# Turned attention rows on VectorE, zeroing from ScalarE's queue, and a plain last write, in a fused attention and mixture-of-experts kernel

## The chip, the cores and the metric

One core of one Trainium2 chip runs the whole program. The metric is the device time of one execution in microseconds (us); the time before is the median of three executions, 692.43 us (691.93 to 693.0).

## What is computed

Decayed linear attention (4 batches, 8 heads, 768 positions, head size 64) gives 3072 tokens of 512 features; each token is then sent to its two best of eight experts, and the two results are added with weights.

```python
for b in range(nb):                       # blocks of 64 positions, per batch and head
    intra = (einsum('bhic,bhjc->bhij', qb, kb) * Dmask) @ vb
    inter = (qb * lam_pow) @ kv_state
    out[b] = intra + inter
    kv_state = lam_block * kv_state + (kb * rev_pow).T @ vb
x = out as [3072, 512]
noisy = x @ w_gate + log1p(exp(x @ w_noise)) * noise
top2, w = two largest of noisy, softmax over the two
for e in range(8):
    out[mask_e] += w_e * (relu(x[mask_e] @ w1[e]) @ w2[e])
```

All arrays are float32. The kernel keeps that precision in the experts by splitting each operand into a high and a low part and adding three products (high·high, high·low, low·high).

## The kernel before, in words

**Attention.** Twelve steps (`for t in range(NST)`), each for two chunks of 128 tokens (tile `a` 0 and 1). A step on TensorE (PE) is, in this order: `products(t-1)` (the gate's logits, L425), `turn_x(t-1)` (L437), `trans_k(t+1)` (L321), `trans_q(t+1)` (L334), `kv(t+1)` (state update, L409), `intra(t)` and `inter(t, 0)` (L377), `scores(t+1)` (L364). PSUM has four rotating buffers called `pS` for transposes, states and scores. ScalarE (ACT) copies the turned keys and queries out (L323, L337), scales the keys (`kdecay`, L349) and copies the outputs out (`evac_o`, L397, into `XO`, features on partitions). VectorE (DVE) multiplies the scores with the decay mask (L367) and the queries with theirs (L341), adds the states (L417), and from step 4 on runs the routing (`routing`), a list of small instructions dealt out by `advance`.

`turn_x(u)` turns the outputs `XO[u]`, which have features on the partitions, into rows of tokens `XC[u]`: eight 128x128 transposes on PE (L437) and two copies by ACT (L438). `store_x(u)` writes these rows to `x_tok` in DRAM, by one DMA of 512 KB on GpSimd's queue for u below 8 and on SyncE's (SP) queue after that (L443). The inputs come by SP's queue: six loads of 256 KB a step (`load`, L160), for keys (`kt`, two buffers), queries (`qt`, two) and values (`vt`, three). A load of step t+3 stands in the program behind the use that frees its buffer in step t. Between them stand the first expert's weights (`load_w`, L770; `LOADS`), which here are in one or two DMAs each of 512 KB. SP's, ACT's and GpSimd's queues are served by the same 16 DMA engines.

**Zeros.** The experts after the first add into `out`, and tokens are written in scattered rows, so `out` is zeroed first by two DMAs on SP's queue (`zero_out`, L1152): 2 MB at step 11 and 4 MB after the first part of expert 0.

**Experts.** Expert 0 runs in three parts of tiles (`PARTS0`); each part is eight first-layer groups (L1037, evacuated by ACT L1043 and DVE L1047) and then the second layer tile by tile (`gemm2`, L1078). Meanwhile GpSimd (POOL) scatters the lists of tokens (`scatter_list`, L634); then SP reads the lists of the next expert back (`load_rec`, L880) and POOL gathers its rows of `x_tok` (`gather_rows`, L889), which PE turns (`trans_rows`, L898). Experts 2 to 7 gather rows, turn them 32x32 on DVE (`turn_rows`, L915) and pass them through DRAM; they form the first layer from seven products of half blocks. Every tile's rows leave through `scatter_out` (L1135): an indirect DMA on POOL's queue, which writes for expert 0 and adds in DRAM for the others. `gemm2` scales the rows on DVE right ahead of it (L1094). After the last tile a loop over overflow tiles follows, which has no turns here.

The order of all engines is the order of the code (`manual_schedule`); waits follow from the data.

## Time and profile before

| what | value |
|---|---|
| median of three executions | 692.43 us |
| the profiled execution: its time, its span | 693.23 us, 691.4 us |
| PE busy, of the span | 671.6 us, 97% |
| DVE, ACT, POOL busy | 482.4, 309.5, 370.0 us |
| DMA | 115.06 MB, mean 166 GB/s |
| granted TensorE clock, mean | 0.994 of full |

Three stretches are to be told apart: the attention (0 to about 140 us), the experts (140 to 683.5 us) and the end (683.5 to 691.4 us, in which PE has nothing left). A busy PE is the bound only where nothing else is busy all the time as well; for the attention the DMA row of the profile has to be read beside it. The profiled execution took 0.80 us more than the median.

### The profile page before, as it was taken

How to read it: one execution, taken by the hardware profiler on the slowest of the kernel's cores; microseconds unless marked ns; L12 is line 12 of the kernel's file. 1: busy time of each engine (PE TensorE's matmuls, PEld its weight loads, DVE VectorE, ACT ScalarE, POOL GpSimd, SP SyncE). 2: the span in 40 equal slices, each digit the busy share in tenths (PEclk: the TensorE clock that was granted, in tenths of full speed). 3: DMA queues.
4: the chain of work that ended last, by engine and by line, in shares of the span. 5: the costliest groups of instructions: out<-in, count | busy, mean ns of one | idle time of the engine just before them, and what ended most of it. 6: DMA issues, size and time to landing. Idle time of an engine off the chain costs nothing.

```text
span 691.4 us, 13961 instructions
## 1 busy us (share of the span) xinstructions
PE 671.6 (97%) x4861; PEld 598.1 (87%) x4861; DVE 482.4 (70%) x1060; ACT 309.5 (45%) x634; POOL 370.0 (54%) x474
## 2 busy tenths in 40 slices
PE   7899999899999999999999999999999999999995
PEld 4788888698898898899989998998898899889984
DVE  6335888878436566789867886889596979588610
ACT  2667786441133332365437434653363356327400
POOL 7111355678854555776358536753773667264332
PEclk9999999999999999999999999999999999999998
DMA  9999999576517437766477547854875576464033
GB/s 205 214 233 262 229 252 250 163 245 163 113 32 221 136 119 171 175 177 191 149 183 188 189 149 178 221 175 142 166 235 158 126 195 189 122 135 116 1 46 40
DMA packets 151901, 115.06 MB, mean 166 GB/s; under 512 B 88063, under 2 KB 123007, under 8 KB 151828
## 3 DMA queue, kind: packets, MB, share of 16 engines
q1 hardware_dynamic: 137636, 84.04, 44.8%
q0 software_dynamic: 13776, 29.57, 20.5%
q8 instruction: 39, 0.64, 0.4%
q10 hardware_dynamic: 416, 0.53, 0.3%
q14 instruction: 34, 0.28, 0.1%
HBM read 77.58 MB, written 37.32 MB: 166 GB/s over the span
## 4 chain that ended last, share of the span: by engine, by line
PE 68%; DVE 12%; issue 8%; POOL 4%; DMA 3%; SPq 2%; ACT 1%; POOLq 1%; DVEq 0%
PE pS L993 15%; PE pKV L1078 13%; PE pO L1078 10%; PE pS L1037 7%; PE pS L1110 5%; PE pS L364 3%; PE pKV L377 2%; POOL lst L634 2%; PE pO L377 2%; SPq L160 2%; PE pR L993 1%; POOL out_dram L1135 1%; DMA xr<-x_tok,rec 1%; DVE ht L1004 1%; PE pS L437 1%
## 5 line engine op out<-in xcount | busy, mean ns | idle before, releaser
L993 PE MATMUL pS<-xa,w 128*128 128x400 f32 (+1 forms) x624 | 158.0, 343 | 0.3 <-ACT gt L1012 0.2
L818 POOL TENSOR_TENSOR wst<-wst 128x256 f32<-128x256 f32 x96 | 96.4, 1016 | 84.1 <-DVE w L810 81.7
L993 PEld LDWEIGHTS pS<-xa,w 128*128 128x128 f32 x624 | 113.2, 188 | 4.6 <-DVE w L810 2.0
L1135 POOL DMA_INDIRECT out_dram<-ot,rec x40 | 73.6, 1839 | 75.5 <-DVE ot L1094 56.2
L1078 PE MATMUL pKV<-w2h,ht 128*128 128x512 f32 x336 | 109.0, 394 | 0.0
L1078 PE MATMUL pO<-w2h,ht 128*128 128x512 f32 x336 | 108.4, 392 | 0.0
L993 PE MATMUL pS<-xb,w 128*128 128x400 f32 (+1 forms) x240 | 81.6, 340 | 0.0
L1078 PEld LDWEIGHTS pKV<-w2h,ht 128*128 128x128 f32 x336 | 63.2, 188 | 14.3 <-DVE gt L1094 0.6
L1078 PEld LDWEIGHTS pO<-w2h,ht 128*128 128x128 f32 x336 | 63.1, 188 | 13.5
L1037 PE MATMUL pS<-xa,w 128*128 128x256 f32 (+2 forms) x440 | 73.5, 316 | 0.8 <-DVE xa L901 0.4
L1037 PEld LDWEIGHTS pS<-xa,w 128*128 128x128 f32 x440 | 65.3, 189 | 4.9 <-DVE xa L901 0.6
L1078 PE MATMUL pKV<-w2l,ht 128*128 128x512 f32 x168 | 65.8, 391 | 0.0
L1078 PE MATMUL pO<-w2l,ht 128*128 128x512 f32 x168 | 65.7, 391 | 0.0
L961 ACT ACTIVATE xa<-wst 128x512 fp32r<-128x512 f32 (+1 forms) x48 | 25.1, 568 | 79.5 <-DVE wst L970 72.3
L810 DVE TENSOR_TENSOR w<-wst,w 128x512 fp32r<-128x512 f32 (+2 forms) x72 | 59.6, 844 | 0.1
L889 POOL DMA_INDIRECT xr<-x_tok,rec x42 | 46.2, 1101 | 19.2 <-issue 6.5
L634 POOL DMA_INDIRECT lst<-recs,dest x48 | 49.7, 1035 | 10.8 <-issue 8.5
L1012 ACT ACTIVATE ot<-pS 128x400 f32<-128x400 f32 (+1 forms) x60 | 29.7, 495 | 48.8 <-PE pS L993 44.6
L808 ACT ACTIVATE w<-wst 128x512 fp32r<-128x512 f32 (+2 forms) x72 | 48.1, 692 | 5.3 <-POOL wst L818 5.2
L1004 DVE SCALAR_TENSOR_TENSOR ht<-ot,ht 128x400 fp32r<-128x400 f32 (+1 forms) x60 | 45.4, 756 | 1.5 <-ACT ht L1001 0.8
L993 PEld LDWEIGHTS pS<-xb,w 128*128 128x128 f32 x240 | 45.0, 188 | 0.6 <-DVE xb L962 0.3
L1043 ACT ACTIVATE ht<-pS 128x256 fp32r<-128x256 f32 (+2 forms) x40 | 17.9, 448 | 59.5 <-PE pS L1037 58.2
(287 smaller groups left out, 1367.0 us busy)
## 6 DMA issues: line engine op xcount, KB each, us to landing
wst<-in_moe_w_dram SPq DMA_DIRECT2D x36, 512.0 KB, 5.4
wst<-in_moe_w_dram SPq DMA_DIRECT2D x32, 256.0 KB, 3.3
kt<-in_k_dram SPq DMA_DIRECT2D x24, 256.0 KB, 5.6
qt<-in_q_dram SPq DMA_DIRECT2D x24, 256.0 KB, 6.7
vt<-in_v_dram SPq DMA_DIRECT2D x24, 256.0 KB, 5.3
wst<-in_moe_w_dram SPq DMA_DIRECT2D x48, 128.0 KB, 3.4
wst<-turned SPq DMA_DIRECT2D x96, 64.0 KB, 2.0
turned<-w1b SPq DMA_DIRECT2D x20, 256.0 KB, 2.8
```

The source lines that it names most:

```text
L634: st = nc.gpsimd.indirect_dma_start(out=lst, out_offset=bass.IndirectOffsetOnAxis(ap=r["dest"][:, i, c:c + 1], axis=0), in_=r["rec"][:, c, ...
L808: nc.scalar.activation(hi[:, ks], src, AF.Copy)
L810: nc.vector.tensor_tensor(lo[:, ks], src, hi[:, ks].bitcast(FT), op=SUB)
L818: g.tensor_tensor(o, x, y, op=op)
L889: nc.gpsimd.indirect_dma_start(out=xrow(e, t)[:size(e, t)], out_offset=None, in_=x_tok[:rows, :], in_offset=bass.IndirectOffsetOnAxis(ap=a ...
L993: nc.tensor.matmul(p, WO[f % 2][:, a, kw, d, :], xo(x, kx, kx + 1)[:, 0, d, :w], start=first and i == 0, stop=i == 5, skip_group_check=True)
L1004: return lambda: nc.vector.scalar_tensor_tensor(hv(e, 1, i, k), src, 0.0, hv(e, 0, i, k).bitcast(FT), op0=OP.max, op1=SUB)
L1012: nc.scalar.activation(banks[m], U, AF.Copy)
L1037: nc.tensor.matmul(p, W1[a][d][:, fs], xt(b, cs)[:, d], start=(d == 0 and i == 0), stop=(d == DB - 1 and i == 2))
L1078: nc.tensor.matmul(p, h, W2[b][f // 2][:, f % 2, :], start=(i == 0), stop=(i == len(TERMS) - 1))
L1110: nc.tensor.matmul(p, W2[b][f // 2][:, f % 2, d * 128:(d + 1) * 128], h, start=(i == 0), stop=(i == len(TERMS) - 1))
L1135: st = nc.gpsimd.indirect_dma_start(out=out, out_offset=bass.IndirectOffsetOnAxis(ap=REC[e, t][:, 0:1], axis=0), in_=o, in_offset=None, bo ...
```

## The change

Five things are changed together.

1. For the first four steps (`BLOCKS = 4`) `turn_x` turns 32x32 blocks on DVE instead of 128x128 on PE. A row of `XC` then lies on 32 partitions at a time with features in the order (32-block, head pair, feature), and `store_x` writes it by four DMAs of 32 partitions with pieces of 512 bytes instead of one DMA with rows of 2 KB. The later steps still use PE, and ACT's copy writes the same new order.
2. `x_tok` so has its features in another order. The first expert's weights are loaded to match: `load_w` takes four DMAs of 32 rows each where it took one or two. `turn_rows` reads its input without a reordering.
3. `out` is zeroed by twelve DMAs of 512 KB on ACT's queue, one behind each first-layer evacuation of expert 0's second part (eight) and the first four of its third part, in place of the two on SP's queue.
4. Ahead of expert 7's second layer POOL gathers the rows of `out` that its last tile will add to, into the tile `zero`.
5. The last tile is scaled and added to these rows on DVE (one SCALAR_TENSOR_TENSOR for one TENSOR_SCALAR) and is then written by an indirect DMA that doesn't add.

```diff
--- before.py
+++ after.py
@@ -67,8 +67,8 @@
 LOADS = {2: [(1, 0)], 3: [(1, 1)], 4: [(1, 2)], 5: [(1, 3)], 9: [(2, 0), (2, 1)], 10: [(2, 2)], 11: [(2, 3)]}
 HIGH = {4: [(1, 0)], 5: [(1, 1)], 6: [(1, 2)], 7: [(1, 3)], 10: [(2, 0), (2, 1)]}
 LOW = {5: [(1, 0)], 6: [(1, 1)], 7: [(1, 2)], 10: [(2, 0)]}
-ZEROS = {11: 8}
 LATE = (6, 7)
+BLOCKS = 4
 MID = 16
 X1 = ((), (), (), (), (0, 1), (2, 3, 4), (5, 6))
 WARM = (10, 1, 1)
@@ -430,18 +430,28 @@
 
     def turn_x(u):
 
-        XC[u] = aw.tile([128, 2, DB, C], FT, name="xc")
+        XC[u] = aw.tile([128, 2, DM], FT, name="xc")
         for a in range(2):
+            if u < BLOCKS:
+                nc.vector.transpose(XC[u][:, a].rearrange("p (i d c) -> p i d c", d=DB, c=32),
+                                    XO[u][:, a].rearrange("p d (i c) -> p i d c", c=32))
+                continue
             p = bank()
             for d in range(DB):
                 nc.tensor.transpose(p[:, d, :], XO[u][:, a, d, :], identf)
-            nc.scalar.activation(XC[u][:, a], p, AF.Copy)
+            nc.scalar.activation(XC[u][:, a].rearrange("p (i d c) -> p d i c", d=DB, c=32),
+                                 p.rearrange("p d (i c) -> p d i c", c=32), AF.Copy)
 
     def store_x(u):
 
         queue = nc.gpsimd if u < NST - 4 else nc.sync
+        if u < BLOCKS:
+            for i in range(4):
+                queue.dma_start(sub(x_tok, 2 * u * C * DM + i * 128, [[DM, 32], [32 * DM, 2 * DB], [1, 128]]),
+                                XC[u][i * 32:(i + 1) * 32].rearrange("p a (i x) -> p (a i) x", x=128))
+            return
         queue.dma_start(x_tok[2 * u * C:2 * (u + 1) * C, :].rearrange("(a p) m -> p a m", a=2),
-                          XC[u].rearrange("p a d i -> p a (d i)"))
+                        XC[u])
 
     def logits(u):
         nonlocal pl
@@ -764,10 +774,9 @@
     def load_w(which, e, j, queue=nc.sync):
         st = next(stage)
         if which == 1:
-            for s in range(2 if j % 2 else 1):
-                r = half(s) if j % 2 else slice(0, 128)
-                src = w1[EXP[e], j * 128 + (64 - r.start if j % 2 else 0):, :][:, :r.stop - r.start, :]
-                queue.dma_start(st[r, None, :], src.rearrange("e p f -> p e f"))
+            for d in range(DB):
+                at = d * 128 + (j ^ 2 * (d % 2)) * 32
+                queue.dma_start(st[d * 32:(d + 1) * 32, None, :], w1[EXP[e], at:at + 32, :].rearrange("e p f -> p e f"))
         else:
             src = w2[EXP[e], j * 256:(j + 1) * 256, :]
             queue.dma_start(st.rearrange("p (e a m) -> p e a m", e=1, a=2),
@@ -913,7 +922,7 @@
         else:
             tr = (zero, WX[0][:, :DM], WX[0][:, DM:])[next(place) % 3][:n, :]
         nc.vector.transpose(tr.rearrange("p (i d c) -> p i d c", d=DB, c=32),
-                            xrow(e, t)[:n, :].rearrange("p (d i c) -> p i d c", d=DB, c=32))
+                            xrow(e, t)[:n, :].rearrange("p (i d c) -> p i d c", d=DB, c=32))
         nc.sync.dma_start(turned[t % 3 if t < NT - 1 else 3][t // 3 % 2, :n, :], tr)
 
     def xturned(t):
@@ -1056,6 +1065,7 @@
 
     ahead = []
     OT = []
+    LAST = E - 1, tile_order(E - 1)[-1]
 
     def ring():
         OT.append(OT.pop(0))
@@ -1091,7 +1101,10 @@
             p = o
         if e in CROSS and n == TS:
             o, p = o.rearrange("p (b d c) -> p b d c", b=DB, c=32), p.rearrange("p (d b c) -> p b d c", b=DB, c=32)
-        nc.vector.tensor_scalar(o, p, w, None, op0=MULT)
+        if (e, t) == LAST:
+            nc.vector.scalar_tensor_tensor(o, p, w, zero, op0=MULT, op1=ADD)
+        else:
+            nc.vector.tensor_scalar(o, p, w, None, op0=MULT)
         if e:
             scatter_out(e, t, o if n < TS or e not in CROSS else o.rearrange("p b d c -> p (b d c)"))
 
@@ -1134,7 +1147,7 @@
         nc.gpsimd.memset(spacer, 0.0)
         st = nc.gpsimd.indirect_dma_start(
             out=out, out_offset=bass.IndirectOffsetOnAxis(ap=REC[e, t][:, 0:1], axis=0), in_=o, in_offset=None,
-            bounds_check=NTOK - 1, oob_is_err=False, **({"compute_op": ADD} if e else {}))
+            bounds_check=NTOK - 1, oob_is_err=False, **({"compute_op": ADD} if e and (e, t) != LAST else {}))
         if t == 0:
             out_st.clear()
         for s in out_st:
@@ -1149,8 +1162,8 @@
     def zero_out(n):
         i = list(itertools.islice(zeros, n))
         if i:
-            nc.sync.dma_start(out[i[0] * 128:(i[-1] + 1) * 128, :].rearrange("(a p) m -> p a m", p=128),
-                              zero[:, None, :].to_broadcast([128, len(i), DM]))
+            nc.scalar.dma_start(out[i[0] * 128:(i[-1] + 1) * 128, :].rearrange("(a p) m -> p a m", p=128),
+                                zero[:, None, :].to_broadcast([128, len(i), DM]))
 
     for t in range(NST):
         u = t + 1
@@ -1169,7 +1182,7 @@
             kv(u)
         if t:
             store_x(t - 1)
-            paced(1, XC[t - 1][:, 1, 0, :])
+            paced(1, XC[t - 1][:, 1, :])
         if t not in LATE:
             kdecay(t + 2)
         if u == NST:
@@ -1204,7 +1217,6 @@
         advance(FILLA.get(t, 18))
         for which, j in LOADS.get(t, []):
             load_w(which, 0, j)
-        zero_out(ZEROS.get(t, 0))
         if t == 2:
             turn_noise()
         if t == 4:
@@ -1256,6 +1268,8 @@
                     finish(2, False)
             if i or f >= 2:
                 paced(1 + (i == 2), ht(0, 0, f, columns(0, t0, n)).bitcast(FT))
+            if i:
+                zero_out(2)
             if i == 1 and f == 2:
                 load_rec(0, 1)
             if i == 2 and f == 2:
@@ -1270,7 +1284,6 @@
                 for j in X1[f - 4]:
                     trans_rows(j, size(1, j))
         if i == 0:
-            zero_out(NTOK // 128)
             advance(50)
         if i == 1:
             which_expert(1, nc.sync)
@@ -1472,6 +1485,10 @@
             step, todo = first_layer(e)
         if e == E - 1:
             nc.gpsimd.drain()
+            nc.gpsimd.indirect_dma_start(
+                out=zero, out_offset=None, in_=out,
+                in_offset=bass.IndirectOffsetOnAxis(ap=REC[LAST][:, 0:1], axis=0),
+                bounds_check=NTOK - 1, oob_is_err=False)
         if e == 1:
             WX.append(wp.tile([128, F], FT, name="w1b"))
             XB.append(hp.tile([128, 6 * 2 * HW], FR, name="xb"))
```

How this moves instructions, at the places that the prediction speaks of. On PE, at the start of an attention step (here the second; `identf` is the identity, `xo` the outputs, `kt` and `qt` keys and queries):

```order
 L377 MATMUL pO<-qTs,S_171 64x128
 L425 MATMUL pR<-xo,wgn 32x256 x4
-L437 MATMUL pS<-identf,xo 128x128 x8
 L321 MATMUL pS<-identf,kt 128x128 x8
 L334 MATMUL pS<-identf,qt 128x128 x8
```

The eight transposes of the outputs are gone, and those of the keys follow the gate's products directly. On DVE, at the same place:

```order
 L367 TENSOR_TENSOR at<-pS,Mk_130 128x512
 L367 TENSOR_TENSOR at<-pS,Mk_131 128x512
+L436 STREAM_TRANSPOSE xc<-xo 128x512 x2
 L341 TENSOR_TENSOR qTs<-pS,QS 128x4x128 x2
 L417 TENSOR_TENSOR S_174<-S_174,pS 128x256
```

Two transposes stand between the masks of the scores and the scaling of the next queries. On POOL, the stores of the first rows between the state updates (S):

```order
 L416 TENSOR_TENSOR S_172<-S_171,QS 128x256
 L416 TENSOR_TENSOR S_173<-S_172,QS 128x256
 L416 TENSOR_TENSOR S_174<-S_173,QS 128x256
-L443 DMA x_tok<-xc 128x2x512
+L450 DMA x_tok<-xc 32x8x128 x4
 L416 TENSOR_TENSOR S_171<-S_170,QS 128x256
```

Each store is four issues in the place of one. On POOL, ahead of expert 7's second layer, before:

```order
L818 TENSOR_TENSOR wst_161<-wst_161 128x2x128 x4
L818 TENSOR_TENSOR wst_162<-wst_162 128x2x128 x4
L846 TENSOR_TENSOR w2l_323<-wst_164,w2h_319 128x1024
L1134 MEMSET spacer 1x1
L1135 DMA out_dram<-ot_2377,rec_6565 3072x512
```

and in the changed kernel:

```order
L827 TENSOR_TENSOR wst_161<-wst_161 128x2x128 x4
L827 TENSOR_TENSOR wst_162<-wst_162 128x2x128 x4
L855 TENSOR_TENSOR w2l_323<-wst_164,w2h_319 128x1024
L1488 DMA zero<-out_dram,rec_6569 128x512
L1147 MEMSET spacer 1x1
L1148 DMA out_dram<-ot_2358,rec_6567 3072x512
```

The gather of the last tile's rows of `out` stands ahead of the expert's first write.

## Rows read from the trace of the kernel before

**Rows 1.** Busy us of each engine in stretches (start:end, length), instructions, PE clock, DMA share, GB/s.
```profile
30.00:40.00 10.00, 10.00 (x156) 8.76 (x155) 4.10 (x7) 7.27 (x20) 0.76 (x1) 1.00 1.08 237
120.00:130.00 10.00, 9.24 (x156) 7.85 (x156) 9.09 (x37) 5.71 (x10) 4.94 (x12) 1.00 0.39 123
130.00:140.00 10.00, 6.74 (x86) 5.28 (x82) 7.14 (x29) 4.03 (x8) 7.91 (x15) 1.00 0.74 241
140.00:150.00 10.00, 10.00 (x100) 9.91 (x101) 6.77 (x27) 5.46 (x12) 6.62 (x9) 1.00 0.66 161
190.00:200.00 10.00, 10.00 (x68) 9.83 (x66) 2.98 (x9) 1.85 (x5) 8.26 (x19) 1.00 0.33 59
```

**Rows 2.** Chain of work that ended last, 36 to 50 us (start, us, what).
```profile
37.80 0.57 PE pR L425 x8
38.37 1.02 PE pS L437 x8
```

**Rows 3.** By line: a DVE block transpose, ACT's and POOL's part in turned rows (ns).
```profile
L915 DVE STREAM_TRANSPOSE w1b<-xr 128x512 f32<-128x512 f32 x20 | 13.9, 696 | 0.0
...
L438 ACT ACTIVATE xc<-pS x24: 592/597/598, 29.6 to 142.5; 128x512 f32<-128x512 f32 x24
...
L443 POOL DMA_DIRECT2D x_tok<-xc x8: 733/742/794, 30.9 to 105.3; - x8
```

**Rows 4.** DMA, 20 to 110 us: queues (packets, MB, share), issues (KB, us to landing).
```profile
q1 hardware_dynamic: 58968, 16.91, 90.8%
q0 software_dynamic: 1307, 4.69, 15.9%
...
vt<-in_v_dram SPq DMA_DIRECT2D x19, 256.0 KB, 4.9
```

**Rows 5.** SP's queue: loads in order of issue (start, us), 59 to 64 and 92 us.
```profile
59.50 2.20 SPq L770 DMA_DIRECT2D wst<-in_moe_w_dram  x2
61.81 1.45 SPq L160 DMA_DIRECT2D kt<-in_k_dram  x2
63.36 4.11 SPq L160 DMA_DIRECT2D qt<-in_q_dram  x2
...
91.94 1.50 SPq L160 DMA_DIRECT2D vt<-in_v_dram  x1
```

**Rows 6.** Timeline, step 8: PE's first state product, and DVE's next masks.
```profile
101.78 0.34 PE L409 MATMUL pS<-vt,kd 128*64 128x64 f32 x4
...
106.95 2.48 DVE L367 TENSOR_TENSOR at<-pS,Mk 128x512 f32<-128x512 f32 x4 [0.56 <-PE pS L364]
```

**Rows 7.** The end: timeline from 682.5 us, and the last write's us to landing.
```profile
683.15 0.40 PE L1078 MATMUL pKV<-w2h,ht 128*128 128x512 f32 x1
683.58 0.75 DVE L1094 TENSOR_SCALAR ot<-pKV,rec 128x512 f32<-128x512 f32 x1 [4.74 <-PE pKV L1078]
684.61 1.56 POOL L1135 DMA_INDIRECT out_dram<-ot,rec  x1 [3.90 <-DVEq L1520]
...
out_dram<-ot,rec POOLq DMA_INDIRECT x1, 4.5
```

**Rows 8.** Indirect writes that don't add (xb), all landings on out, a DVE form.
```profile
L1135 POOL DMA_INDIRECT out_dram<-xb,recz x5: 985/998/1890, 230.9 to 241.8; - x5
...
DMA to landing us min/median/max: 2.7/5.1/7.6
...
out_dram<-xb,recz POOLq DMA_INDIRECT x5, 3.6
...
L1047 DVE SCALAR_TENSOR_TENSOR ht<-pS,ht 128x512 fp32r<-128x512 f32 x8 | 5.5, 692 | 9.7 <-ACT ht L1043 9.7
```

**Rows 9.** Gather at 207 us (chain), PE's wait for it, issues of zeros.
```profile
207.65 3.47 DMA xr<-x_tok,rec
...
PEld pS L898 <- DMA xr<-x_tok,rec: 0.3, 1, 0.3
...
L1152 SPq DMA_DIRECT2D out_dram<-zero x2: 520/698/877, 132.8 to 148.8; - x2
```

## The prediction

> **What bounds the kernel now.** I read first the table of busy time by stretches [rows 1], then the chain of waits through one attention step [rows 2], then the DMA queues and SP's issues [rows 4, 5], and last the end of the timeline [rows 7]. From 30 to 40 us PE is busy 10.00 of 10.00 us, at the full clock (1.00), while DVE has 4.10, ACT 7.27 and POOL 0.76; a reader would stop there and call the attention bound by PE. The DMA share in the same row is 1.08, though, and SP issues its loads one behind the other with next to nothing between (59.50 + 2.20 = 61.70, the next at 61.81; + 1.45 = 63.26, the next at 63.36) [rows 5]. So PE and the DMA engines are both full there: loads are not issued when a buffer comes free but when the queue takes them. From 120 to 140 us the row changes: PE has 9.24 and 6.74 of 10, DVE 9.09 and 7.14; routing on DVE paces the end of the attention. From 140 us PE is at 10.00 again. Then only the last 8 us are without PE: its last product starts at 683.15 and takes 0.40; DVE's scaling (0.75), POOL's part of the write (1.56) and its landing follow [rows 7], and the span ends at 691.4 us.
>
> **PE in four steps.** The eight transposes L437 are 1.02 us of the chain in a step [rows 2]. Four steps lose them: 4 x 1.02 = 4.1 us off PE. What comes in their place lies beside PE. DVE gets two block transposes of 0.696 us a step [rows 3], 1.4 us on an engine with 4.10 of 10 busy; they stand ahead of the next queries' scaling, which waits for PE's transposes anyway. ACT loses two copies of 0.597. POOL issues four DMAs where it issued one: 3 x 0.742 = 2.2 us more a step, on an engine with 0.76 busy [rows 1, 3]. What waits behind them on POOL is the next step's state update, several us away. If this cover were missing, the most it could cost is the 1.4 us of DVE a step.
>
> **The loads.** Steps that are shorter by 1.02 us want their inputs earlier, and the DMA engines have no time to give. The latest one I take is the second half of the values for step 8's product: issued at 91.94 [rows 5], landing 4.9 us later by the median of these loads [rows 4], so at 96.84; PE takes it at 101.78 [rows 6]. That is 4.94 us of margin, and PE will want it 4.1 us earlier, at 97.68. Alone, that still fits.
>
> But the change also gives the DMA engines more to do before that. The stores of rows now move 512-byte pieces instead of 2 KB ones. No row shows such pieces written, so I bound them. GpSimd's queue moved 4.69 MB in 15.9% of 16 engines over 90 us [rows 4], that is 90 x 0.159 = 14.3 us of all engines, or 1.60 us for a store of 0.524 MB. SP's queue with its 256-byte pieces took 0.908 x 90 = 81.7 us for 16.91 MB, or 2.53 us for 0.524 MB. A store of 512-byte pieces costs between the two, 0 to 0.93 us more. By a line through the time of a piece (256 bytes: 81.7 x 16 / 58968 = 22 ns; 2 KB: 14.3 x 16 us over 4.69 MB / 2048, 100 ns) a 512-byte piece takes 33 ns, 1024 of them on 16 engines 2.1 us: 0.5 us more, an estimate. Four stores give 2.1 us (bounds 0 and 3.7). The load then lands at 96.84 + 2.1 = 98.9 and PE, which wants it at 97.7, waits 1.3: of 4.1 us, **2.8 us** stay.
>
> The Trainium skill has a rule against this estimate ("DMA: Bandwidth & Descriptors", section Specifications): transfers in pieces of 512 bytes or more run at line rate, and only below that is there a read-modify-write. By it the four stores would cost nothing more and the full 4.1 us would stay. No run here shows such pieces yet.
>
> The split of the first expert's weights into four DMAs adds 10 issues on SP in these steps (6 before, 16 now). With bytes and row length unchanged I take them at nothing, because an issue there mostly waits for the queue; if each adds what a free issue costs (0.52 us, the least of the zeroing rows [rows 9]), it is 5.2 us, and the loads would take the whole gain. That is the other bound.
>
> The shift then has to pass the stretch where DVE paces. At 106.95 DVE still waits 0.56 us for PE's scores [rows 6], so it is not behind there, and all it does after that moves with PE. From 140 us on PE is full and carries the shift to the end.
>
> **The end.** The last write doesn't add any more. Writes of expert 0, which don't add either, take 0.998 us of POOL instead of 1.56 and land 3.6 us after their issue instead of 4.5 [rows 7, 8]: 0.9 us. DVE's new form reads one tensor more; the nearest form (128x512 from PSUM and SBUF) takes 0.692 us against 0.75 [rows 7, 8], another 0.05. I take **1.0 us**. Bounds: the least landing on `out` is 2.7, a gain of 1.8; POOL can also take 1.89, and then there is nothing. The gather of these rows stands on POOL behind the work before expert 7's second layer, with PE busy for long after; it costs nothing.
>
> **Zeros.** Their removal from SP's queue frees DMA time where nothing on the path waits for it (0.39 of the engines at 120 to 130 us, PE held by DVE). In the new place the engines are at 0.33 [rows 1] and ACT at 1.85 of 10; twelve issues of 0.5 to 0.9 us [rows 9] lie beside PE. I take 0, with the third rival as the bound. The other edits (order of ACT's copy, `turn_rows` without reordering) change no count of work and cost nothing.
>
> **Sum.** 2.8 + 1.0 = 3.8 us. Against the profiled execution, 693.23 - 3.8 = 689.4 us; that execution is 0.8 above the median, so the median I predict is 692.43 - 3.8 = **688.6 us**.
>
> **Rivals.**
> First, PE keeps all it gains: 4.1 + 1.0 = 5.1, 687.3 us. For it: every DMA of this mix might overlap better than my sums, and the margin of 4.94 is above 4.1. Against: a DMA share of 1.08 and SP without a pause.
> Second, the loads take it all: if stores and extra issues together delay the values by 4.94 us or more, PE waits for what it saved, and only the end is left: 691.4 us. For it: bounds of 3.7 and 5.2 us for these two. Against: SP's issues are long because the queue is full, so shorter ones need not add.
> Third, slower: the zeros hold up the gather for expert 1. The rows of the second tile come at 207.65 + 3.47 = 211.12, and PE already waits 0.3 us for them [rows 9]; behind this gather stands a chain of list scatter, list load and gather, all through the same engines. The last four pieces go out with the third part of expert 0, in the stretch 190 to 200 us [rows 1]; at 1.60 us for 0.524 MB they are 6.4 us of transfer. If they stand ahead of that chain, PE waits 6.4 us: 688.6 + 6.4 = 695.0. It decides against the change once more than 3.8 us of zeros are still waiting when the lists go out. For it: no slack. Against: only 0.33 of the engines is in use there [rows 1], and the four come one behind each first-layer group, not all at once.
> That the transposes stay on PE is excluded by the order shown above; that the last write waits for its gather is excluded by the time between.
>
> **How the numbers follow.** Chances: my forecast (687.8 to 690.6) 0.50, the first rival 0.24, the second 0.18, the third 0.08. The range holds the forecast, the first rival with the better end (692.43 - 4.1 - 1.8 = 686.5) and the second (691.4): 686.4 to 691.6; of the third it leaves out nearly all. A measurement of this kernel can tell about 0.2%, 1.4 us, from no change: faster is below 691.05, slower above 693.8. Forecast and first rival are faster; of the second I count 0.05 as faster and 0.13 as the same; of the third 0.01 the same and 0.07 slower: 0.79, 0.14, 0.07.
>
> **What would show it.** In the new profile: steps 1 to 4 shorter by about 1 us each in PE's chain, with L321 directly behind L425; the state product of step 8 (101.78 now) at about 99, and in front of it or of the steps around it a PE wait for `vt`, `qt` or `kt` of 1 to 2 us that is not there now. No such wait and a start near 97.7 would be the first rival; a start near 101 the second. GpSimd's queue should show a share of the engines that grows by some 2 us. At the end, POOL's part near 1.0 us, landing near 3.6, and 1 us less from the last product to the span's end. At the gather, PE's wait should stay under 1 us; several us there would be the third rival. The prediction is wrong if PE's shift at 140 us isn't between 1.5 and 4 us, or if a stall between 160 and 230 us takes it back.

## The result, and the profile after

The changed kernel takes 702.44 us (median of 6 executions, 698.34 to 705.55) beside 692.73 us of the kernel before: ratio 1.012 (1.0091 to 1.015). Run again later it gave 1.0133 (1.0086 to 1.0179). The prediction was 688.6 us, 0.6% faster; the kernel is 1.2% slower. The kernel before itself had medians from 692.7 to 701.4 us beside the six sets of runs (on several chips), so every run below is given by its ratio to the kernel before that ran beside it; a range in brackets is the 95% interval.

The profiled execution of the changed kernel took 705.55 us, its span is 703.8 us: 12.4 us more than the span before, and 3.1 us more than its own median. Where the 12.4 us are is read from the stretches of 10 us (columns as in [rows 1]):

```profile
70.00:80.00 10.00, 8.07 (x122) 6.79 (x118) 8.43 (x45) 7.78 (x18) 4.43 (x5) 1.00 0.83 220
80.00:90.00 10.00, 8.65 (x140) 7.32 (x136) 7.91 (x20) 4.92 (x13) 4.42 (x5) 1.00 0.89 217
100.00:110.00 10.00, 8.24 (x112) 7.40 (x111) 2.60 (x10) 8.58 (x22) 7.15 (x8) 0.83 1.14 268
190.00:200.00 10.00, 10.00 (x59) 9.17 (x58) 4.14 (x9) 0.87 (x2) 8.46 (x17) 1.00 0.86 121
200.00:210.00 10.00, 10.00 (x67) 9.78 (x66) 3.34 (x12) 3.34 (x7) 3.86 (x9) 1.00 1.07 241
210.00:220.00 10.00, 4.88 (x22) 3.75 (x21) 3.02 (x3) 1.18 (x2) 3.35 (x3) 0.84 0.46 111
220.00:230.00 10.00, 7.91 (x28) 6.17 (x27) 1.38 (x2) 3.08 (x4) 4.37 (x6) 0.65 0.64 228
```

The same stretches in the kernel before, the first, the third and the fifth:

```profile
70.00:80.00 10.00, 10.00 (x160) 8.76 (x158) 8.58 (x38) 7.93 (x19) 3.60 (x4) 1.00 0.99 243
100.00:110.00 10.00, 10.00 (x159) 8.76 (x158) 5.55 (x17) 6.95 (x18) 8.66 (x13) 1.00 1.13 268
200.00:210.00 10.00, 10.00 (x58) 9.12 (x57) 2.23 (x8) 3.55 (x6) 3.89 (x4) 1.00 0.18 39
```

It has PE busy 10.00 of 10.00 in each of the first three stretches. So there are two new holes: one in the attention between 70 and 110 us, one at the gather for expert 1 between 210 and 230 us; in both the granted clock falls as well. In 190 to 210 us the DMA engines are at 0.86 and 1.07; before, they were at 0.33 [rows 1] and 0.18 in these stretches.

Taking PE's marks one by one against the kernel before: the products of logits (L425) of step 5 start at 63.63 us (before 67.92), those of step 9 at 111.99 (before 108.33), the last at 140.37 (136.71); the transposes for the third part of expert 0 at 187.61 (183.94); PE's last product at 696.83 (683.15 [rows 7]). The shift is -4.3, +3.7, +3.7, +3.7 and +13.7 us, and the end then gives 1.3 back. So this execution lost 8 us between steps 5 and 9, 10.0 us at the gather, and won 1.3 at the end: 3.7 + 10.0 - 1.3 = 12.4.

**The attention.** ScalarE's and PE's timelines from 71 us (start, us, what, idle time before it and what ended it):

```profile
71.14 2.44 ACT L349 ACTIVATE kd<-kt,pwt 128x128 f32<-128x128 f32 x8 [3.20 <-DMA kt<-in_k_dram]
73.49 0.57 ACT L397 ACTIVATE xo<-pO 128x512 f32<-128x512 f32 x1
```
```profile
74.60 0.65 PE L377 MATMUL pKV<-qTs,S 64*64 64x128 f32 x8 [1.60 <-ACT xo L397]
90.48 1.14 PE L334 MATMUL pS<-identf,qt 128*128 128x128 f32 x8 [1.82 <-ACT xc L442]
```

ScalarE stands 3.20 us at the scaling of the keys (`kdecay`, L349) until the keys have landed. Behind it in its queue stand the copies of the outputs (L397) and of the turned rows (L442), and PE waits for those. The wait view (in total, times, longest) has it for ScalarE from 30 to 140 us:

```profile
ACT kd L349 <- DMA kt<-in_k_dram: 12.2, 7, 3.2
```

In the profile before, L349 waited for no load in this time. PE's holes in the three rows above are 5.0 us (1.93, 1.35 and 1.76). Behind the last of them comes a stretch at a lower granted clock (0.52 and 0.63 of full, the last column but two), which by an estimate from these two rows costs another 1.7 us (0.48 and 0.37 of 2 us each):

```profile
104.00:106.00 2.00, 2.00 (x38) 2.00 (x38) 0.84 (x2) 1.23 (x4) 0.81 (x1) 0.52 1.10 272
106.00:108.00 2.00, 2.00 (x28) 2.00 (x26) 0.60 (x2) 2.00 (x8) 1.61 (x4) 0.63 1.21 223
```

SP's issues in this stretch:

```profile
71.84 4.74 SPq L779 DMA_DIRECT2D wst<-in_moe_w_dram  x4
76.63 2.87 SPq L1224 DMA_DIRECT2D lst<-linit  x4
80.48 1.02 SPq L160 DMA_DIRECT2D kt<-in_k_dram  x2
```

The DMA engines are not full all the time here: just ahead of this load of keys they are at 0.39 and 0.24, while SP waits for loads of its own that it issued earlier (rows of busy time, then SP's wait view from 30 to 115 us):

```profile
78.00:80.00 2.00, 1.67 (x36) 1.36 (x36) 1.47 (x6) 1.49 (x4) 0.00 (x0) 1.00 0.39 96
80.00:82.00 2.00, 2.00 (x42) 1.83 (x40) 1.90 (x7) 0.13 (x1) 1.27 (x2) 1.00 0.24 66
```
```profile
SPq L1224 <- DMA vt<-in_v_dram: 1.2, 1, 1.2
SPq L160 <- DMA wst<-in_moe_w_dram: 0.9, 1, 0.9
```

So these keys are late by SP's queue as well as by full engines. What that costs is answered below by a run with as few loads of weights as before.

**The gather.** Timelines of POOL (last list scattered; first gather), SP (weights and list of expert 1) and PE:

```profile
203.53 0.98 POOL L644 DMA_INDIRECT lst<-recs,dest  x1 [0.16 <-issue]
215.89 1.03 POOL L898 DMA_INDIRECT xr<-x_tok,rec  x1 [11.38 <-DMA rec<-lst]
```
```profile
189.18 18.39 SPq L779 DMA_DIRECT2D wst<-in_moe_w_dram  x16
213.56 0.35 SPq L889 DMA_DIRECT2D rec<-lst  x1
```
```profile
219.45 1.12 PE L907 MATMUL pS<-identf,xr 128*128 128x128 f32 x4 [5.12 <-DMA xr<-x_tok,rec]
222.65 1.11 PE L907 MATMUL pS<-identf,xr 128*128 128x128 f32 x4 [2.09 <-DMA xr<-x_tok,rec]
230.72 0.60 PE L907 MATMUL pS<-identf,xr 128*128 128x128 f32 x4
```

The last scatter is issued at 203.53 and the list read at 213.56, 10.0 us later; before it was 4.1 us:

```profile
199.81 0.98 POOL L634 DMA_INDIRECT lst<-recs,dest  x1 [0.16 <-issue]
203.90 0.34 SPq L880 DMA_DIRECT2D rec<-lst  x1
```

PE waits 5.12 and 2.09 us. The other 2.8 of the 10 us fit the lower clock: four transposes take 1.12 us after the wait and 0.60 at 230.72. In the same stretch the zero pieces took long as well (DMA view, 195 to 222 us: KB each, us to landing; over all twelve pieces it is 7.7):

```profile
out_dram<-zero ACTq DMA_DIRECT2D x4, 512.0 KB, 11.2
```

**The end.** It answers to [rows 7]:

```profile
696.83 0.39 PE L1088 MATMUL pKV<-w2h,ht 128*128 128x512 f32 x1
```
```profile
697.26 0.75 DVE L1105 SCALAR_TENSOR_TENSOR ot<-pKV,rec,zero 128x512 f32<-128x512 f32 x1 [4.74 <-PE pKV L1088]
```
```profile
698.29 1.05 POOL L1148 DMA_INDIRECT out_dram<-ot,rec  x1 [3.90 <-DVEq L1537]
```

POOL's part is 1.05 us for 1.56, and from PE's last product to the span's end it is 6.97 us for 8.25.

### The profile page after: what moved, and what is told of

Same layout as the page of the kernel before. It is cut to its first block, busy times and chain, and to the rows that moved or that the text cites. A ratio compares the mean times of both kernels' runs of the same rounds, so it can differ in the third digit from the quotient of the medians.

```text
span 703.8 us, 13983 instructions
## 1 busy us (share of the span) xinstructions
PE 672.2 (96%) x4829; PEld 596.6 (85%) x4829; DVE 487.4 (69%) x1068; ACT 305.7 (43%) x626; POOL 374.7 (53%) x487
## 5 line engine op out<-in xcount | busy, mean ns | idle before, releaser
L1148 POOL DMA_INDIRECT out_dram<-ot,rec x40 | 72.1, 1803 | 74.6 <-DVE ot L1107 43.3
```

The costliest lines, as they stand in the source:

```text
L1148: st = nc.gpsimd.indirect_dma_start(out=out, out_offset=bass.IndirectOffsetOnAxis(ap=REC[e, t][:, 0:1], axis=0), in_=o, in_offset=None, bo ...
```

## The experiments

Starting point: what is slow are the zeros (theory A at the gather) and something that makes the keys late (the split of the weights into 32-row loads, or the 512-byte stores, or the loads as such). The diffs are against the kernel named; a line `...` stands for code left out.

### The zeros

**Zeros alone**, in the kernel before:

```diff
-        zero_out(ZEROS.get(t, 0))
...
+            if i:
+                zero_out(2)
...
-            zero_out(NTOK // 128)
```
(and `nc.scalar` for `nc.sync` in `zero_out`). Expected: 

> The kernel before with the zeros alone changed: twelve pieces on ScalarE's queue. Theory A (the zeros take the DMA engines while expert 1's weights and lists are loaded, so that PE waits for expert 1's gathered rows): a PE wait at L898 between 205 and 225 us of 3 to 8 us where there is 0.3 now, and 3 to 10 us more in all, 696 to 703. Rival B (the zeros are harmless; the stall in the changed kernel comes from expert 1's weights, which are loaded in 16 pieces there): no such wait, within 1.5 us of the kernel before.

Measured: ratio 1.0089 (1.0061 to 1.0117). The rows of the gather:

```profile
199.23 0.98 POOL L633 DMA_INDIRECT lst<-recs,dest  x1 [0.16 <-issue]
211.15 1.05 POOL L888 DMA_INDIRECT xr<-x_tok,rec  x1 [10.93 <-DMA rec<-lst]
```
```profile
214.58 1.11 PE L897 MATMUL pS<-identf,xr 128*128 128x128 f32 x4 [4.56 <-DMA xr<-x_tok,rec]
217.91 1.12 PE L897 MATMUL pS<-identf,xr 128*128 128x128 f32 x4 [2.21 <-DMA xr<-x_tok,rec]
```

Theory A holds: the zeros make this stall without any help. The last four pieces go out between 192 and 198 us, expert 1's weights at 185 to 192, and the DMA engines stay full until 204 us:

```profile
196.00:200.00 4.00, 4.00 (x30) 4.00 (x29) 1.37 (x5) 1.06 (x3) 3.35 (x9) 1.00 1.05 214
200.00:204.00 4.00, 4.00 (x29) 4.00 (x28) 1.41 (x6) 0.88 (x2) 0.22 (x1) 1.00 1.12 218
204.00:208.00 4.00, 4.00 (x20) 3.36 (x19) 0.56 (x2) 2.33 (x3) 0.00 (x0) 1.00 0.33 97
```

The last scatter, issued at 199.23, is through only after they empty; the list, whose read waits for it, is read at 208.80. The kernel before has the engines at 0.04 and 0.01 in the first two of these stretches.

**Zeros put back** in the changed kernel. Expected: 

> The changed kernel with the zeros put back as they were (two DMAs on SyncE's queue). Theory A: the stall at the gather goes, which is about 10 of the changed kernel's us; left are the attention's loss of 3.7 us and the end's gain of 1.3, so 692.7 + 2.4 = 695. Rival B: the stall stays, 700 to 703.

Measured: ratio 0.997 (0.995 to 0.9989), 1.5% below the changed kernel; the stall at the gather is gone (PE waits 0.3 us there). I had expected 2.4 us above the kernel before, for the loss in the attention; it is 0.3% below, so that loss doesn't show in the time. All that makes the change slower lies in the zeros and what they meet.

**Zeros early**, in the kernel before, with this one line against the run with the zeros alone:

```diff
-            if i:
+            if i < 2 and f >= 2:
                 zero_out(2)
```
Expected: 

> The kernel before with the twelve zero pieces on ScalarE's queue, but behind the groups 2 to 7 of expert 0's first and second part instead of the second and third. Theory A (what hurts is that the pieces are still moving when expert 1's weights and the last lists go out): the wait at L897 is under 1 us, the last list lands within 5 us of its issue, and the time is within 1.5 us of the kernel before. Rival E (what hurts is the queue: pieces on ScalarE's queue and loads on SyncE's hold each other up wherever they stand): PE still waits 3 us or more at the gather or in the first part of expert 0, 3 to 7 us slower than before.

Measured: ratio 0.9974 (0.995 to 0.9997). PE's wait for expert 1's rows, in place of the two above:

```profile
211.76 0.66 PE L897 MATMUL pS<-identf,xr 128*128 128x128 f32 x4 [0.80 <-DMA xr<-x_tok,rec]
213.23 0.66 PE L897 MATMUL pS<-identf,xr 128*128 128x128 f32 x4 [0.81 <-DMA xr<-x_tok,rec]
```

Same queue, same pieces, no loss: rival E falls. What costs is that the pieces are in front of expert 1's weights and last lists. The Trainium skill says why another queue is no help by itself ("DMA: Bandwidth & Descriptors", section Issuing engines are not separate DMA queues): transfers started by different engines run on the same 16 DMA engines and interleave there. These runs agree, with a zero piece that lands 7.7 us after its issue in the changed kernel as a whole and 11.2 us beside the weights.

**Early in the changed kernel**, the same one line. Expected: 

> The changed kernel with one line altered: the twelve zero pieces stand behind the groups 2 to 7 of expert 0's first and second part (still on ScalarE's queue). If the zeros cost only by lying in front of expert 1's weights and lists, nothing is left of the loss: the ratio to the kernel before is 0.994 to 0.998, as with the zeros put back. Rival: the 16 loads of expert 1's weights still meet the last pieces, ratio 1.000 to 1.005.

Measured: ratio 0.9983 (0.9957 to 1.0008), PE's longest wait at the gather 0.9 us. The changed kernel beside it on this chip, expected as 

> The changed kernel once more, beside the others on this chip: 1.009 to 1.015 of the kernel before, PE waiting 6 us or more for expert 1's rows.

It gave 1.0133. One line takes 1.5% away.

**Expert 1's weights in 6 loads instead of 16**, in the changed kernel (other values for expert 1). Expected: 

> The changed kernel with expert 1's first-layer weights alone loaded as before, in 6 DMAs instead of 16 (their rows then stand in another order than the features of x, so expert 1 computes other values). Theory A2 (the 16 small loads, caught between the zero pieces on the same semaphores, add to the stall): the list for expert 1 is read 3 us or more earlier after the last scatter than in the changed kernel (10 us there), and the ratio to the kernel before falls from 1.012 to 1.005 to 1.008. Rival H (the bytes of the zeros alone make the stall): the ratio stays above 1.010.

Measured: ratio 1.0052 (1.0022 to 1.0082), as theory A2 said, and its interval is apart from both of the changed kernel. The list is read 5.1 us after the last scatter (211.87, 216.93). But the run with zeros alone has 6 loads too and 9.6 us there, and PE waits 6.8 us for expert 1's rows in it and 2.4 in this one. So the ratio says that the 16 loads cost some 0.7% beside the zeros (without the zeros 0.01%, next section); by which wait isn't shown.

### The attention

**Split alone**, in the kernel before:

```diff
...
+            for d in range(DB):
+                at = j * 128 + (d + 2 * (j % 2)) % DB * 32
+                queue.dma_start(st[d * 32:(d + 1) * 32, None, :], w1[EXP[e], at:at + 32, :].rearrange("e p f -> p e f"))
```
Expected: 

> The kernel before with the first layer's weights of experts 0 and 1 loaded by four DMAs of 32 rows each, in the old row order, and nothing else. Theory A (the split is what makes the loads of keys late, ScalarE waits for them in L349 and PE for ScalarE): L349 waits for kt by 8 to 13 us in all where it waits for no load now, PE is 5 to 8 us late at the end of the attention, 697 to 701. Rival B (the stores in pieces of 512 bytes are what fills the DMA engines): no wait of L349 for kt, 692 to 694.

Measured: ratio 1.0005 (0.9984 to 1.0027). L349 waits 5.5 us for keys, but PE ends the attention where it did. Theory A's price for the split falls, and so does rival B, which had no wait at all. Nor does it take the split to make the keys late: with the attention and the weights' loads as before, L349 waits 5.1 us for keys in the run with the end alone, 5.0 with the zeros early and 2.6 with the zeros alone (all below or above), and none in the profile before. One of these waits, in the run with the end alone, behind which PE stands 2.1 us for ScalarE's copy:

```profile
115.95 2.45 ACT L349 ACTIVATE kd<-kt,pwt 128x128 f32<-128x128 f32 x8 [3.77 <-DMA kt<-in_k_dram]
```

**Turns without the split** (weights whole, zeros put back, from the changed kernel). Expected: 

> The changed kernel with the zeros put back and the weights of experts 0 and 1 loaded whole as before (so their rows stand in another order than the features of x, and these two experts compute other values). Turns on VectorE, stores in 512-byte pieces and the plain last write are left. Theory A: the attention keeps most of its 4.1 us and the end gives 1.3, so 687.3 to 689.5, and L349 waits for kt by under 2 us. Rival B: L349 waits as in the changed kernel and the time is 694 to 696.

Measured: ratio 0.9969 (0.9952 to 0.9987), within 0.0001 of the run with the split. Neither theory met it: the split is innocent, and the 4 us are not there either. L349 waits 5.6 us for keys. The DMA engines are full here (1.02 and 1.14 from 70 to 90 us), where the changed kernel has 0.83 and 0.89; so SP's waits in that profile are not what takes the 4 us.

**And with whole stores**:

```diff
-        if u < BLOCKS:
-            for i in range(4):
...
-            return
```
Expected: 

> As the run with weights whole and zeros put back, but the first four stores go out as one DMA each with rows of 2 KB, as before the change (the rows then lie in x_tok in a wrong order of blocks, so the experts read other values; the bytes are the same). Theory C (the 512-byte pieces and their four DMAs cost the DMA engines what the loads then lack): step 5 starts 4 us earlier than before the change and steps 9 to 12 keep at least 3 of it; 2 to 4 us below the run with 512-byte stores. Theory D (the loads were the bound together with PE already, whatever the stores cost): steps 9 to 12 start within 1 us of the kernel before, and the time is within 1 us of the run with 512-byte stores.

Measured: ratio 0.9976 (0.9947 to 1.0005), so taking the 512-byte pieces away brings nothing, as theory D said. What they cost the DMA engines can be read from GpSimd's queue from 29 to 75 us (packets, MB, share of 16 engines), first with the pieces, then whole, then in the kernel before:

```profile
q0 software_dynamic: 820, 2.31, 17.8%
```
```profile
q0 software_dynamic: 582, 2.12, 12.5%
```
```profile
q0 software_dynamic: 576, 2.10, 14.8%
```

17.8% of 46 us are 8.2 us, 3.5 us a MB; 12.5% are 5.8 us, 2.7 a MB; the kernel before has 3.2 a MB. A store of 0.524 MB in pieces so costs 0.2 to 0.4 us more. Over all profiles it is 2.7 to 3.2 us a MB in the nine kernels with whole stores and 3.2 to 3.6 in the ten with pieces. The rule of the Trainium skill that the prediction weighed ("DMA: Bandwidth & Descriptors", section Specifications: pieces of 512 bytes run at line rate) would have it at 0; these rows have a little more.

**Keys scaled later on ScalarE** (zeros put back, `LATE = (4, 5, 6, 7, 8, 9)` for `(6, 7)`). Expected: 

> The changed kernel with the zeros put back, and the scaling of keys (L349's group) behind the copies of the outputs on ScalarE in steps 4 to 9, where it stood so in steps 6 and 7 alone. Theory F (PE loses its time because ScalarE stands at the late keys with PE's copies behind it): PE's waits for xo and xc (2.4 and 2.3 us in the run without this edit) fall under 1 us, and the time is 2 to 4 us below that run. Theory D (the loads bound the steps, so the wait only moves): PE waits as long, for vt, kt or qt or for the scaled keys, and the time is within 1 us of that run.

Measured: ratio 0.9987 (0.996 to 1.0014). PE's wait for `xo` at L377 is gone, the one for `xc` is 3.2 us in place of 2.3: the wait only moved. Theory F falls.

**Less to load.** The two runs that decide it fill expert 0's first-layer weights with zeros instead of loading them:

```diff
-        if which == 1:
+        if which == 1 and e == 0:
+            nc.gpsimd.memset(st, 0.0)
+        elif which == 1:
```
With the turns (weights of expert 1 whole, zeros put back): 

> The run with turns on VectorE and expert weights whole, and with expert 0's first-layer weights left out (four tiles filled with zeros by GpSimd in steps 2 to 5, so 2 MB fewer through the DMA engines there). Theory D (the loads bind the attention together with PE, so what PE saves turns into waits): with room in the DMA engines PE keeps its 4 us; step 9 starts 3 us or more before that of the same kernel without turns and weights, and the time is 2.5 to 4 us below it. Rival G (the turns on VectorE bring a wait of their own): the two are within 1.5 us of each other.

Without them: 

> The kernel before with expert 0's first-layer weights left out in the same way. Theory D: L349 waits for no keys, PE is full from step 2 to step 9, and the time is 0 to 2 us below the kernel before, since PE binds as soon as the loads don't. If it fell by 4 us or more, the loads alone would have been the bound of the kernel before.

Measured: 0.9919 (0.9893 to 0.9945) with the turns, 0.9991 (0.9965 to 1.0017) without; 0.72% apart, 5.0 us of 701. The end is 1.3 of these, and PE's last products of the attention are 3.4 us earlier. L349 hardly waits for keys, 0.2 us with the turns and not at all without; ScalarE's wait view names its own copy of the queries instead (here with the turns):

```profile
ACT kd L350 <- ACT qT L338: 0.9, 3, 0.3
ACT kd L350 <- DMA kt<-in_k_dram: 0.2, 1, 0.2
```

The starts of PE's products of logits (first of a step, us) put all of it into one table; where a row names several runs, its numbers stand in their order:

| kernel | step 5 | step 9 | last |
|---|---|---|---|
| before | 67.92 | 108.33 | 136.71 |
| zeros alone; split alone | 67.21; 67.20 | 107.62; 108.93 | 135.98; 136.55 |
| end alone; zeros early | 67.26; 67.08 | 107.87; 109.12 | 138.95; 137.22 |
| changed; again | 63.63; 63.93 | 111.99; 107.34 | 140.37; 135.75 |
| zeros put back; early | 63.75; 64.32 | 110.72; 112.46 | 139.08; 140.83 |
| turns without the split; stores whole; keys later | 65.17; 63.77; 64.02 | 109.30; 109.21; 108.95 | 137.69; 137.58; 137.34 |
| no weights, with turns | 64.04 | 104.48 | 134.32 |
| no weights, without turns | 67.42 | 107.90 | 137.77 |

Every kernel with the turns is 2 to 4 us ahead at step 5, and at step 9 it is where the others are (within 0.3 us) or behind them, unless 2 MB of loads are missing; then it keeps 3.4 us to the end. So theory D is shown: the loads take what the turns save. Whether they do so by the 16 engines alone or also by the order and waits of SP's queue, these runs don't separate, since leaving weights out relieves both. The first four rows also show how much one execution differs from the next: 3.0 us at the last step with the old turns, and 4.6 us between the two profiles of the changed kernel (140.37 and 135.75), so its +3.7 is nothing that every execution has.

### Weights behind the last inputs

If the loads bind, 1 MB less among them should let the turns pay, in a kernel that computes everything. **Moved**, with turns, end and early zeros:

```diff
-LOADS = {2: [(1, 0)], 3: [(1, 1)], 4: [(1, 2)], 5: [(1, 3)], 9: [(2, 0), (2, 1)], 10: [(2, 2)], 11: [(2, 3)]}
+LOADS = {2: [(1, 0)], 3: [(1, 1)], 8: [(1, 2)], 9: [(1, 3), (2, 0)], 10: [(2, 1)], 11: [(2, 2), (2, 3)]}
```
(`HIGH`, `LOW` and one more split to match). Expected: 

> As the run with the zeros early, and two of the four first-layer weight tiles of expert 0 (1 MB) loaded behind the last queries, keys and values instead of among them, with their splits moved to steps 9 to 11. Theory D (the loads take what PE saves by the turns): step 9 starts 2 to 4 us earlier than in the run without the move, and if the splits find room on ScalarE and GpSimd the ratio falls to 0.989 to 0.994. Rival: VectorE's and GpSimd's routing in steps 10 to 12 gets the splits in its way and takes the gain back; step 9 starts earlier, the end of the attention doesn't, ratio 0.995 to 1.000.

Measured: step 9 starts at 104.38, 8 us before the run without the move and 3 us before the earliest of all runs with the turns and the loads in their old places, but the last products at 137.84; ratio 0.9984 (0.9959 to 1.0009), as without the move (0.9983). The first half of theory D and the rival's second half. Not the routing, as the rival had it, but the moved weight itself took it back, on ScalarE:

```profile
119.62 1.06 ACT L851 ACTIVATE w<-wst 128x1024 fp32r<-128x1024 f32 x1 [4.32 <-DMA wst<-in_moe_w_dram]
```

**Moved alone**, in the kernel before. Expected: 

> The kernel before with the two weight tiles of expert 0 moved behind the last queries, keys and values, and nothing else. Theory D: without the turns PE is the bound as soon as the loads are not, so there is little to gain, ratio 0.997 to 1.001; L349 waits for no keys. If the loads alone were the bound before, the ratio would be below 0.996.

Measured: ratio 1.0057 (1.0037 to 1.0077): the move costs 4 us by itself, which I had not expected. ScalarE waits 4.3 us for the moved weight here too, and 0.9 for keys. So in the run above the turns, the end and the zeros together bring 0.7%, and the move takes it.

**Splits a step later.** Expected: 

> The run with the two weight tiles moved, where ScalarE then stood 4.3 us for the first moved tile in step 9 and PE behind it; now both splits stand one step later (steps 10 and 11), and the first low part of the second layer behind the attention. Theory D: step 9 starts at 104 to 105 as there, ScalarE has no wait for weights, the attention ends 1.5 to 4 us earlier than in the kernel before (133 to 135 for the last logits products), ratio 0.990 to 0.995. Rival: the last keys or the routing on VectorE hold steps 10 to 12 as before, and the ratio stays 0.996 to 1.000.

This kernel takes the low part of one second-layer weight tile from other data. Measured: step 9 at 105.24, the last products at 133.62, 3.1 us before those of the kernel before: PE's gain does reach the end of the attention. But the ratio is 1.004 (1.0023 to 1.0056): the transposes for expert 0's second part start at 158.95, only 0.6 us early, so 2.5 us are gone in its first part, where one split now stands. Both theories had a lower ratio. PE also waits 2.6 us for expert 1's rows; where the rest goes was not followed up.

### The end

**End alone**, in the kernel before. Expected: 

> The kernel before with the end alone changed: rows of out gathered ahead of expert 7's second layer, added on VectorE, written without adding. My theory: POOL's part of the last write 1.05 us instead of 1.56, from the last product to the span's end about 1.2 us less, and 1.0 to 1.5 us less in all. Rival: the gather or the wait of the last scaling for it costs something elsewhere and the whole is within 0.5 us of the kernel before.

Measured: ratio 0.9975 (0.9949 to 1.0001), and from the last product (685.89) to the span's end (692.9) 7.0 us for 8.25. The mechanism is shown, 1.24 us; the ratio is of that size, though its interval just reaches 1.

**End and early zeros**, in the kernel before. Expected: 

> The kernel before with the two parts that did not lose: the gathered and plain last write, and the twelve zero pieces on ScalarE's queue behind the groups of expert 0's first and second part. Expected from the two runs apart: 1.2 us from the end and 0 to 1 from the zeros, ratio 0.996 to 0.9985. Rival: the zeros in the first part delay the gathers there and take the end's gain, ratio 1.000 or above.

Measured: 0.9973 (0.9943 to 1.0003), no more than either alone. Of the kernels that compute what the kernel before computes, two have an interval below 1: the changed one with its zeros put back (0.997) and the kernel before with early zeros (0.9974). None of them beats the kernel before by more than 0.3%.

## Why the prediction was wrong, step by step

- **PE in four steps** (4.1 us): right in kind. Step 5 starts 4.29 us earlier; 0.80 of that was there at the first products already (27.5 for 28.3), so the turns gave 3.5, 0.87 us a step and not 1.02. DVE and POOL covered what came in their place.
- **The loads** (2.8 of 4.1 stay): wrong, and it is the outcome of the second rival, to which I gave 0.18, though not by its reason: without stores in pieces and without the split the 4 us are not there either. The step that failed is "The latest one I take is the second half of the values", with its margin of 4.94 us. Those values landed later than the median said, at 98.8 in the trace before (the last of the sixteen marks of their semaphore), so their margin was 3.0 us. And the keys had less: in the two rows behind this paragraph, SP issues the halves for step 10 from 93.55 on, their last marks stand at 99.8 and 101.5, and L349, each of whose instructions reads both halves, starts at 103.03. That margin is 1.5 us, against 4.1 that PE wanted. And the reader of the keys is ScalarE, in whose queue PE's copies stand behind, so PE is stopped by a load that it doesn't read. What the runs show in place of the 2.8 us: the last products of the attention come 1.0 us earlier to 4.1 later than in the profile before in the table's kernels with the turns and all loads in their places, and 3.4 us earlier than without the turns once 2 MB of loads are missing. The price of the stores (0.5 us each) was nearly right, 0.2 to 0.4, but taking them away brought nothing (0.9976 for 0.9969).

```profile
93.55 3.95 SPq L160 DMA_DIRECT2D kt<-in_k_dram  x2
```
```profile
103.03 2.45 ACT L349 ACTIVATE kd<-kt,pwt 128x128 f32<-128x128 f32 x8 [0.28 <-ACT qT L337]
```

- **The split** (nothing, with 5.2 as its bound): right for the time of the attention, 1.0005 alone, though SP's issues do not only wait for a full queue: in the changed kernel SP stood while the engines were at 0.39 and 0.24. Beside the zeros it costs about 0.7% more, which no step had.
- **The end** (1.0 us): right, 1.3 in the changed kernel, 1.24 alone.
- **The zeros** (0): wrong, the larger of the two errors, and it is the third rival, at 0.08. The step that failed is "In the new place the engines are at 0.33". That row was taken from the kernel before, where expert 1's weights (2 MB) had gone through before 195 us; behind the first eight pieces SP issues them from 189.18 on (before from 181.28), beside the last four, and the same stretch is then at 0.86 and 1.07. The point from which the rival was to decide (3.8 us of zeros still waiting when the lists go out) was passed: when the last scatter goes out at 203.53, none of the last four pieces has landed (their last marks stand at 206.1 to 214.3). Its price of 6.4 us was short of the 10.0 of the profile: PE's waits are 7.2, and the lower clock behind them fits the other 2.8.
- **Sum**: 3.8 us less was expected. In the profile it is 3.7 more in the attention, 10.0 more at the gather and 1.3 less at the end. By the ratio it is 1.2%, 8.3 us of 692.4: gather and end alone make 8.7, so if the gather cost the other executions as much as the profiled one, the attention gained or lost next to nothing on their average.

## What to carry to other kernels

Where two resources bind together, as PE and the loads here, expect work taken from one to become waiting until the other is relieved too; look for the load with the least margin among all its readers, above all a reader in an in-order queue with other engines' work behind it. A stretch that looks empty in the profile before is not empty for a transfer that moves there, if the earlier pieces of the same transfer push its present tenants into it: lay out the queue's whole order again, not the share of one row. A wait of PE is to be priced with the slower clock behind it (here 7.2 us of waits and 2.8 behind them).

## What the runs showed of the hardware

After PE's wait of 5.12 us at the gather the granted clock is at the lower of its two levels, 1.2 for 2.4 GHz (the row of 218 to 220 us has 0.50), and it is back by 230 us:

```profile
218.00:220.00 2.00, 0.55 (x3) 0.56 (x4) 0.78 (x1) 0.00 (x0) 1.54 (x2) 0.50 0.65 209
```

A scatter of lists that lands 4.1 us after its issue takes 10 beside 4 MB of zeros and weights on other queues. And four kernels with the attention and its loads as before reach the last products of the attention between 135.98 and 138.95 us, in profiles taken on several chips; the latest of them is the one with the 3.77 us wait for keys shown above, but why its keys came later there is not shown. A change of a few tenths of a per cent can't be read from one profile here.
